# Three partial matmuls of a split product, with the two that use the weights' high part put next to each other

## The chip, the cores and the metric

The kernel runs on one core of a Trainium2 chip. The metric is device time in microseconds; the kernel before takes 951.2 us (median of three runs, 950.86 to 952.58).

## The reference

Sliding-window attention with a distance bias, and a gated feed-forward network behind it, on 8 batches of 576 tokens, 8 heads of 64, d_model 512, d_ff 1536:

```python
scores = scale * q @ k.T + bias          # window of 128, causal
attn   = softmax(scores)
x      = (attn @ v)  -> [4608, 512]
gate   = 1 / (1 + exp(-(x @ w_gate)))
out    = (gate * (x @ w_val)) @ w_out
```

All inputs and outputs are float32.

## The kernel before

**Split products.** The feed-forward matmuls take operands in a rounded 32-bit format that TensorE handles in one pass. To keep float32 accuracy, every operand is cut into two: a high part (the value rounded to that format, written by a copy) and a low part (the value minus its high part, written by a subtraction that reads the high part). A product is then the sum of three matmuls into one PSUM bank: high x high, and the two mixed ones (high part of one operand, low part of the other). The weights are TensorE's stationary operand and the activations its moving one, so each matmul is a pair of instructions: a weight load (PEld in the profile) and the matmul itself (PE).

**Three places** issue such triples. `project` in `gates1` (L695) does the first four of twelve d_ff chunks as a plain product, 8 projections of 4 triples for each of 5 token blocks of 512, in between the attention's own matmuls. `product` in `gates2` (L780) does the other chunks with a seven-product scheme (sums of sub-blocks, buffers cxA, cxB, cxC), 384 or 512 tokens wide. `product` in `results` (L1064) does the out projection with a scheme of 15 products, 512 wide, from four buffers (three in cxA, one in cxC) used in turn.

**Where the parts come from.** `parts` (its copy is recorded at L286 or L287, its subtraction at L296) writes the high part and then the low part. Each is written anew when a new block or sub-block comes, and then has to wait until the matmuls that read the old one are through. `x1` (tile x in the trace) holds one token block for L695; there is one copy of it.

**What sets the order.** Nothing is issued as the code is written. Every step is entered in a `Graph` with an engine, an assumed cost, what it reads and writes and a wish time (`want`). `order` then goes through the entries as a greedy planner: it takes the entry that can start first (in buckets of 0.05 us), among equal ones that with the lower wish time, and so fixes the order in which each engine's instructions are issued. A table (`SHIFTS`) moves the wish times of groups of entries. In `gates2` and `results` the six matmuls of two triples are ONE entry, which reads all four parts:

```python
g.add("PE", 6 * (N / 2400 + 0.0133), six, [("xc", k, 0), ("xc", k, 1), ("w2", i, 0, wa), ("w2", i, 1, wa)], ...
```

In `project` every matmul is an entry of its own, which reads one part of the weights and one of x, with the highest wish time of all (it goes where nothing else can start):

```python
g.add("PE", n / 2400 + 0.014, one, [("w1", kind, wi, i), (("xhi", "xlo")[x], c)], keys_of(s), 1.0e6)
```

Semaphores between engines are put in by the framework, from the instructions as they are issued: each instruction waits for the writers of what it reads itself. TensorE's waits stand on the weight load of the pair.

Of the kernel before, what the change touches and what calls it, by code (L numbers as in the profile page):

```python
# [259 lines left out]
def act_cost(n, psum=False):  # L260
    return (0.05 if psum else 0.1) + n * 0.00084
# [3 lines left out]
def attention_gated_ffn(ctx: ExitStack, tc: tile.TileContext, qd, kd, vd, wg, wv, wo, out):  # L265
# [409 lines left out]
    def gates1(t0, n):  # L675
        F = FIRST
        xr = lambda: xrow()[:, :, 0:n]
        a = t0
        while t0 and a < t0 + n:
            b = a // S  # L680
            e = min((b + 1) * S, t0 + n)
            move(lambda a=a, e=e: xr()[:, :, a - t0:e - t0],
                 lambda b=b, a=a, e=e: xs[b][:, :, a - b * S:e - b * S].rearrange("c p t -> p c t"),
                 [("xs", b, p) for p in range(NPAIR)], [("xr", c, a > t0) for c in range(KC)], F, 2 * (e - a))
            a = e
        for c in range(KC if t0 else 0):
            parts(lambda c=c: x1(0)[:, c, 0:n], lambda c=c: x1(1)[:, c, 0:n], lambda c=c: xr()[:, c], n,
                  [("xr", c, e) for e in range(2)], ("xhi", c), ("xlo", c), F)

        def project(kind, i):  # L690
            s = bank()
            for c in range(KC):
                for k, (wi, x) in enumerate(((0, 0), (1, 0), (0, 1))):
                    def one(c=c, k=k, wi=wi, x=x):
                        nc.tensor.matmul(psum(s)[:, 0:n], w1(kind, wi)[:, i, c * P:(c + 1) * P], x1(x)[:, c, 0:n],  # L695
                                         start=(k == 0 and c == 0), stop=(k == 2 and c == KC - 1))
                    g.add("PE", n / 2400 + 0.014, one, [("w1", kind, wi, i), (("xhi", "xlo")[x], c)], keys_of(s), 1.0e6)
            return s

        for i0 in range(0, FC1, GRP):  # L700
            grp = range(i0, min(FC1, i0 + GRP))
            for i in grp:
                s = project("g", i)
                g.add("ACT", act_cost(n, psum=True), lambda s=s, i=i: nc.scalar.activation(sgate(i % GRP)[:, 0:n], psum(s)[:, 0:n], AF.Tanh, scale=0.5),
                      keys_of(s), [("sg", i % GRP)], F)
            for i in grp:
                s, r = project("v", i), spills[0] % NRING1
                spills[0] += 1
                h = lambda r=r: ring[:, r * NB:r * NB + n]
                g.add("DVE", dve_cost(n, psum=True), lambda s=s, i=i, h=h: nc.vector.scalar_tensor_tensor(  # L710
                    h(), sgate(i % GRP)[:, 0:n], 1.0, psum(s)[:, 0:n], op0=ALU.add, op1=ALU.mult), [*keys_of(s), ("sg", i % GRP)], [("rg1", r)], F)
                spill(h, ("rg1", r), i, t0, n)
# [33 lines left out]
    def gates2(t):  # L746
        F = FIRST + (1 if t else 0.4)
        N, t0 = HALVES[t], EDGE[2 * t]
        xr = lambda: xrow()
        x = lambda h, k: (lambda: xr()[:, 2 * k:2 * k + 2, h * N2:h * N2 + N])  # L750
        for h in range(2):
            a = t0 + h * N
            while a < t0 + (h + 1) * N:
                b = a // S
                e = min((b + 1) * S, t0 + (h + 1) * N)
                move(lambda a=a, e=e, h=h: xr()[:, :, h * (N2 - N) + a - t0:h * (N2 - N) + e - t0],
                     lambda b=b, a=a, e=e: xs[b][:, :, a - b * S:e - b * S].rearrange("c p t -> p c t"),
                     [("xs", b, p) for p in range(NPAIR)], [("xr", k, (h, a > t0 + h * N)) for k in range(2)], F, 2 * (e - a))
                a = e
        xk = {(h, k): [("xr", k, (h, e)) for e in range(2)] for h in range(2) for k in range(2)}  # L760
        m = 2 * N
        mixed = mix(lambda k, val, reads: parts(lambda: combo(k, 0)[:, :, 0:N], lambda: combo(k, 1)[:, :, 0:N], val, m, reads, ("xc", k, 0), ("xc", k, 1), F),
            x, xk, m, F)
        have = set()

        def chunk(i):
            bx, by, bz = bank(), bank(), bank()
            sa, su, sp_ = scratch(), scratch(), scratch()
            a1, u2, p5 = (lambda s=s: ring2(s)[:, 0:N] for s in (sa, su, sp_))
            sg = [lambda h=h: sgate(h)[:, 0:N] for h in range(2)]  # L770
            bk = lambda b: (lambda: mm[b][:, 0:N])

            def product(k, b, start, wk):
                while k not in have:
                    have.add(next(mixed))

                def six():
                    for c in range(2):
                        for j, (xp, wp) in enumerate(((0, 0), (0, 1), (1, 0))):
                            nc.tensor.matmul(mm[b][:, 0:N], w2t(i, wp)[:, wk, c * P:(c + 1) * P], combo(k, xp)[:, c, 0:N],  # L780
                                             start=(start and c == 0 and j == 0), stop=(c == 1 and j == 2), skip_group_check=True)
                wa = 0 if wk < 2 else 2
                g.add("PE", 6 * (N / 2400 + 0.0133), six, [("xc", k, 0), ("xc", k, 1), ("w2", i, 0, wa), ("w2", i, 1, wa)],
                      [("mm", b)], 1.0e6)

            def total(o, b, a, reads, writes, okeys):
                g.add("DVE", dve_cost(N, psum=True), lambda: nc.vector.tensor_tensor(o(), bk(b)(), a(), op=ALU.add),  # L787
                      [("mm", b), *reads] if okeys else reads, writes, F)

            def gate(b, h):  # L790
                g.add("ACT", act_cost(N, psum=True), lambda: nc.scalar.activation(sg[h](), bk(b)(), AF.Tanh, scale=0.5),  # L791
                      [("mm", b)], [("sg", h)], F)

            def gated(o, val, reads, key, h, psum):
                g.add("DVE", dve_cost(N, psum, True), lambda: nc.vector.scalar_tensor_tensor(
                    o(), sg[h](), 1.0, val(), op0=ALU.add, op1=ALU.mult), [("sg", h), *reads], [key], F, port=not psum)
                spill(o, key, chunk_of(i), t0 + h * N, N)

            ka, ku, kp = (("rg", s) for s in (sa, su, sp_))
            product(0, bx, True, 0)  # L800
            copy(a1, bk(bx), N, [("mm", bx)], [ka], F, psum=True)
            yield
            product(3, bz, True, 3)
            copy(p5, bk(bz), N, [("mm", bz)], [kp], F, psum=True)
            yield
            product(4, bx, False, 4)
            copy(u2, bk(bx), N, [("mm", bx)], [ku], F, psum=True)
            yield
            product(1, by, True, 1)
            total(bk(by), by, a1, [ka], [("mm", by)], False)  # L810
            gate(by, 0)
            yield
            product(5, bx, False, 5)
            total(p5, bx, p5, [], [kp], True)
            yield
            product(2, bz, False, 2)
            total(bk(bz), bz, u2, [ku], [("mm", bz)], False)
            gated(u2, bk(bz), [("mm", bz)], ku, 0, True)
            yield
            product(6, bx, False, 6)  # L820
            gate(bx, 1)
            gated(p5, p5, [], kp, 1, False)

        return chunk
# [128 lines left out]
    def results(wsrc):  # L953
# [97 lines left out]
        def product(t, e, k, at):  # L1051
# [6 lines left out]
            for i in two:  # L1058
                b = banks_[z][i]
                for a, c in halves(t, k, i) if e else ((0, NB),):  # L1060
                    def six(b=b, i=i, a=a, c=c):
                        for d in range(2):
                            for j, (xp, wp) in enumerate(((0, 0), (0, 1), (1, 0))):
                                nc.tensor.matmul(mm[b][:, a:c], wot(n, wp)[:, 2 * e + d, i * P:(i + 1) * P], pieces[q](xp)[:, d, a:c],  # L1064
                                                 start=(k in fresh and e == d == j == 0), stop=(e == 1 and d == 1 and j == 2),
                                                 skip_group_check=True)
                    g.add("PE", 6 * ((c - a) / 2400 + 0.0133), six,
                          [("hc", q, 0), ("hc", q, 1), ("wo", n, 0), ("wo", n, 1)] + [("mm", b)] * (a > 0), [("mm", b, 1) if a else ("mm", b)], 1.0e6)
# [3 lines left out]
        for kind, t, e, what, at in plan():  # L1072
            if kind == "wload":
                wsplit(what, at, wsrc)
            elif kind == "load":
                k, b = int(what[1]), int(what[2]) + 3 * t
# [3 lines left out]
            elif kind == "add":  # L1080
                x, y, o = at
# [189 lines left out]
```

## Time and profile before

| | |
|---|---|
| median of three runs | 951.2 us |
| the profiled execution: time, span in the trace | 951.76 us, 949.8 us |
| TensorE: matmuls, weight loads | 6586, 6586 |
| TensorE busy with matmuls, with loads | 941.6 us, 796.4 us |
| VectorE, ScalarE, GpSimd busy | 820.4, 541.4, 153.8 us |

The profiled execution's span is the time from its first to its last instruction; 1.96 us of its time lie around it. A matmul's record runs until its results are out, so consecutive ones overlap, and a mean of some 390 ns is not the distance from one to the next: that is the length of a dense stretch through the matmuls in it. By line and place in time there are three stages: attention with L695 in its gaps (to about 290 us), L780 (to about 700 us), L1064 (to the end).

### The profile page before, as it was taken

How to read it: one execution, taken by the hardware profiler on the slowest of the kernel's cores; microseconds unless marked ns; L12 is line 12 of the kernel's file. 1: busy time of each engine (PE TensorE's matmuls, PEld its weight loads, DVE VectorE, ACT ScalarE, POOL GpSimd, SP SyncE). 2: the span in 40 equal slices, each digit the busy share in tenths (PEclk: the TensorE clock that was granted, in tenths of full speed). 3: DMA queues.
4: the chain of work that ended last, by engine and by line, in shares of the span. 5: the costliest groups of instructions: out<-in, count | busy, mean ns of one | idle time of the engine just before them, and what ended most of it. 6: DMA issues, size and time to landing. Idle time of an engine off the chain costs nothing.

```text
span 949.8 us, 18733 instructions
## 1 busy us (share of the span) xinstructions
PE 941.6 (99%) x6586; PEld 796.4 (84%) x6586; DVE 820.4 (86%) x2022; ACT 541.4 (57%) x1364; POOL 153.8 (16%) x321
## 2 busy tenths in 40 slices
PE   8999999999999999999999999999999999999998
PEld 7888887788888889999988888888888888888886
DVE  7998989986879998796969939895899999999985
ACT  8999988887745654443545425342455435444432
POOL 5665556563400000000001000000000000000000
PEclk9999999999999999999999999999999999999999
DMA  7766768765426436567374422543587795597542
GB/s 265 257 227 231 258 212 274 242 211 194 149 72 210 155 125 207 179 219 242 115 244 167 153 81 72 194 146 132 195 274 256 229 327 174 186 329 245 155 134 89
DMA packets 101294, 185.78 MB, mean 196 GB/s; under 512 B 9680, under 2 KB 37456, under 8 KB 101200
## 3 DMA queue, kind: packets, MB, share of 16 engines
q1 hardware_dynamic: 101200, 184.58, 58.7%
q8 instruction: 52, 0.85, 0.4%
q14 instruction: 42, 0.34, 0.1%
HBM read 128.45 MB, written 56.10 MB: 194 GB/s over the span
## 4 chain that ended last, share of the span: by engine, by line
PE 96%; DVE 1%; DMA 1%; ACT 1%; issue 0%; SPq 0%; POOL 0%; DVEq 0%; ACTq 0%
PE mm L780 44%; PE mm L1064 26%; PE mm L695 12%; PE mm L502 5%; PE mm L643 5%; PE mm L575 4%; PE mm L620 1%; DVE pb L533 1%; PE mm L563 1%; DMA qr<-in_q_dram 0%; ACT pb L536 0%; DMA hs<-ring 0%; DVE mm L512 0%; SPq L291 0%; DVE st L551 0%
## 5 line engine op out<-in xcount | busy, mean ns | idle before, releaser
L286 ACT COPY ring<-mm 128x512 f32<-128x512 f32 (+1 forms) x177 | 97.1, 559 | 165.8 <-PE mm L780 109.6
L695 PE MATMUL mm<-x,wl 128*128 128x512 f32 x480 | 133.6, 410 | 0.0
L589 POOL TENSOR_SCALAR_AFFINE_SELECT pt<-both 128x384 f32<-128x384 f32 (+1 forms) x256 | 114.9, 479 | 96.2 <-ACT both L286 83.3
L780 PE MATMUL mm<-cxB,wh 128*128 128x512 f32 (+1 forms) x504 | 117.1, 374 | 0.2 <-ACT ring L286 0.2
L780 PE MATMUL mm<-cxA,wh 128*128 128x512 f32 (+1 forms) x504 | 117.2, 374 | 0.0
L536 ACT ACTIVATE pb<-pb,st 128x128 f32<-128x128 f32 x288 | 112.5, 394 | 5.2 <-DVE st L533 5.0
L780 PEld LDWEIGHTS mm<-cxB,wh 128*128 128x128 f32 x504 | 92.7, 188 | 14.5 <-ACT ring L286 0.5
L780 PEld LDWEIGHTS mm<-cxA,wh 128*128 128x128 f32 x504 | 92.7, 188 | 14.2 <-DVE wh L296 0.2
L695 PEld LDWEIGHTS mm<-x,wl 128*128 128x128 f32 x480 | 84.2, 188 | 18.4 <-issue 2.2
L1064 PE MATMUL mm<-cxA,wl 128*128 128x512 f32 x416 | 99.2, 389 | 0.0
L791 ACT ACTIVATE sg<-mm 128x512 f32<-128x512 f32 (+1 forms) x96 | 53.7, 564 | 75.8 <-PE mm L780 48.2
L1064 PE MATMUL mm<-cxA,wh 128*128 128x512 f32 (+1 forms) x384 | 94.4, 387 | 0.0
L1064 PEld LDWEIGHTS mm<-cxA,wl 128*128 128x128 f32 x416 | 78.1, 188 | 16.2
L787 DVE TENSOR_TENSOR mm<-mm,ring 128x512 f32<-128x512 f32 (+1 forms) x96 | 62.1, 650 | 28.2 <-PE mm L780 21.1
L1064 PEld LDWEIGHTS mm<-cxA,wh 128*128 128x128 f32 x384 | 71.9, 188 | 14.7
L780 PE MATMUL mm<-cxB,wl 128*128 128x512 f32 (+1 forms) x360 | 82.4, 367 | 0.0
L780 PE MATMUL mm<-cxA,wl 128*128 128x512 f32 (+1 forms) x360 | 81.9, 367 | 0.0
L780 PEld LDWEIGHTS mm<-cxB,wl 128*128 128x128 f32 x360 | 65.9, 188 | 8.6
L780 PEld LDWEIGHTS mm<-cxA,wl 128*128 128x128 f32 x360 | 65.8, 188 | 8.6
L420 DVE SCALAR_TENSOR_TENSOR work<-work 128x512 int32<-128x512 int32 x104 | 71.6, 702 | 0.4
L502 PE MATMUL mm<-kr,qr 64*64 64x192 f32 (+2 forms) x1408 | 61.4, 304 | 0.9 <-DMA qr<-in_q_dram 0.9
L502 PEld LDWEIGHTS mm<-kr,qr 64*64 64x64 f32 x1408 | 49.2, 133 | 9.9 <-issue 4.6
(143 smaller groups left out, 1665.7 us busy)
## 6 DMA issues: line engine op xcount, KB each, us to landing
hs<-ring SPq DMA_DIRECT2D x84, 256.0 KB, 2.4
hb<-hs SPq DMA_DIRECT2D x38, 512.0 KB, 5.3
work<-hs SPq DMA_DIRECT2D x29, 512.0 KB, 4.6
kr<-in_k_dram SPq DMA_DIRECT2D x31, 384.0 KB, 4.4
xr<-hs SPq DMA_DIRECT2D x23, 512.0 KB, 5.4
work<-in_moe_w_gate_dram SPq DMA_DIRECT2D x20, 512.0 KB, 4.2
work<-in_moe_w_val_dram SPq DMA_DIRECT2D x20, 512.0 KB, 4.4
qr<-in_q_dram SPq DMA_DIRECT2D x31, 320.0 KB, 5.0
```

Source lines behind the costliest of these rows:

```text
L286: g.add("ACT", act_cost(n, psum), lambda: nc.scalar.copy(out(), src()), reads, writes, want, release=release, guard=guard, ways=[("DVE", d ...
L420: g.add("DVE", dve_cost(DM, two=True), lambda word=word, scalar=scalar, o0=o0: nc.vector.scalar_tensor_tensor(bits(), wraw(s)[:, :, word], ...
L502: nc.tensor.matmul(sp[v.at][col, j, c0:c0 + n], qraw(u)[row, i // 2, col], kraw(u)[row, k1:k1 + n], start=True, stop=True)
L536: g.add("ACT", 0.39, lambda: nc.scalar.activation(pb()[:, e], pb()[:, e], AF.Exp, bias=st()[:, e:e + 1], scale=-1.0, accum_out=st()[:, 3 + ...
L575: nc.tensor.transpose(tp[:, e], pb()[:, e], ident)
L589: nc.gpsimd.affine_select(pt(u)[:, f0:f0 + 2 * m_ - 1:2, h * D:h * D + D], both().rearrange("p a (h q) -> p (a h) q", q=D)[:, c0:c0 + m_], ...
L643: nc.tensor.matmul(to[e * D:(e + 1) * D], vraw(u)[row, c], seen[row, o + t0:o + t1], start=(k, e) not in begun, stop=jj + 2 > NBLK - 1, sk ...
L695: nc.tensor.matmul(psum(s)[:, 0:n], w1(kind, wi)[:, i, c * P:(c + 1) * P], x1(x)[:, c, 0:n], start=(k == 0 and c == 0), stop=(k == 2 and c ...
L780: nc.tensor.matmul(mm[b][:, 0:N], w2t(i, wp)[:, wk, c * P:(c + 1) * P], combo(k, xp)[:, c, 0:N], start=(start and c == 0 and j == 0), stop ...
L787: g.add("DVE", dve_cost(N, psum=True), lambda: nc.vector.tensor_tensor(o(), bk(b)(), a(), op=ALU.add), [("mm", b), *reads] if okeys else r ...
L791: g.add("ACT", act_cost(N, psum=True), lambda: nc.scalar.activation(sg[h](), bk(b)(), AF.Tanh, scale=0.5), [("mm", b)], [("sg", h)], F)
L1064: nc.tensor.matmul(mm[b][:, a:c], wot(n, wp)[:, 2 * e + d, i * P:(i + 1) * P], pieces[q](xp)[:, d, a:c], start=(k in fresh and e == d == j ...
```

## The change

In each of the three places the second and the third matmul of a triple change places. Before, the weights of the three are high, low, high, and the activations high, high, low. After, the weights are high, high, low, and the activations high, low, high. The same three products are summed into the same bank; the counts of instructions as written are the same.

```diff
         def project(kind, i):
-                for k, (wi, x) in enumerate(((0, 0), (1, 0), (0, 1))):
+                for k, (wi, x) in enumerate(((0, 0), (0, 1), (1, 0))):
...
                 def six():                                   # gates2
-                        for j, (xp, wp) in enumerate(((0, 0), (0, 1), (1, 0))):
+                        for j, (xp, wp) in enumerate(((0, 0), (1, 0), (0, 1))):
...
                     def six(b=b, i=i, a=a, c=c):             # results
-                            for j, (xp, wp) in enumerate(((0, 0), (0, 1), (1, 0))):
+                            for j, (xp, wp) in enumerate(((0, 0), (1, 0), (0, 1))):
```

(`wi` and `wp` pick the part of the weights, `x` and `xp` that of the activations; 0 is the high part.)

## Rows read from the trace of the kernel before

**Rows 1.** The page: busy time by engine; granted clock in 40 slices.
```profile
PE 941.6 (99%) x6586; PEld 796.4 (84%) x6586; DVE 820.4 (86%) x2022; ACT 541.4 (57%) x1364; POOL 153.8 (16%) x321
...
PEclk9999999999999999999999999999999999999999
```

**Rows 2.** The page: the chain that ended last, by engine and line.
```profile
PE 96%; DVE 1%; DMA 1%; ACT 1%; issue 0%; SPq 0%; POOL 0%; DVEq 0%; ACTq 0%
PE mm L780 44%; PE mm L1064 26%; PE mm L695 12%; PE mm L502 5%; PE mm L643 5%; PE mm L575 4%; PE mm L620 1%; DVE pb L533 1%; PE mm L563 1%; DMA qr<-in_q_dram 0%; ACT pb L536 0%; DMA hs<-ring 0%; DVE mm L512 0%; SPq L291 0%; DVE st L551 0%
```

**Rows 3.** Stretches: busy us of each engine (instructions), granted clock, DMA share.
```profile
60.00:290.00 230.00, 230.00 (x2858) 186.03 (x2857) 197.40 (x940) 190.71 (x710) 114.57 (x244) 1.00 0.63 207
290.00:700.00 410.00, 409.84 (x1964) 358.69 (x1963) 340.85 (x566) 187.00 (x316) 3.75 (x2) 1.00 0.50 166
700.00:950.00 250.00, 246.06 (x1092) 203.79 (x1090) 230.32 (x231) 109.11 (x132) 0.00 (x0) 1.00 0.66 219
```

**Rows 4.** Waits of the matmuls: us in total, times, longest.
```profile
PE mm L780 <- ACT ring L286: 0.2, 1, 0.2
```

**Rows 5.** Stretches inside the two product stages, columns as in Rows 3.
```profile
740.00:840.00 100.00, 100.00 (x443) 82.80 (x442) 95.48 (x96) 44.89 (x55) 0.00 (x0) 1.00 0.73 239
390.00:440.00 50.00, 49.84 (x288) 49.52 (x287) 45.44 (x89) 22.27 (x44) 0.00 (x0) 1.00 0.63 208
```

**Rows 6.** The whole span, lines 695, 780 and 1064 each alone.
```profile
0.00:950.00 950.00, 133.57 (x480) 84.18 (x480) 1.00 0.59 196
0.00:950.00 950.00, 422.14 (x2016) 368.72 (x2016) 1.00 0.59 196
0.00:950.00 950.00, 245.03 (x1086) 203.15 (x1086) 1.00 0.59 196
```

**Rows 7.** Line 355 alone: duration min/median/max ns, first and last start.
```profile
L355 PEld LDWEIGHTS mm<-ident x40: 186/192/333, 3.1 to 18.0; 128*128 128x128 f32 x40
L355 PE MATMUL mm<-ident x40: 275/275/421, 3.3 to 18.1; 128*128 128x128 f32 x40
```

**Rows 8.** Tile x, 36 to 290 us: idle ahead of its loads, times.
```profile
  DVE x L296: 0.7, 2
...
  DVE wl L296: 0.2, 1
```

**Rows 9.** In order of time, 47.8 to 49.9 us: start, us, engine, line.
```profile
47.46 2.62 PE L695 MATMUL mm<-x,wl 128*128 128x512 f32 x10
...
47.72 0.42 DVE L287 CAST x<-xt 128x512 fp32r<-128x512 f32 x1
...
48.17 1.00 DVE L296 TENSOR_TENSOR x<-xt,x 128x512 fp32r<-128x512 f32 x1
```

**Rows 10.** In order of time, 160.5 to 163.2 us.
```profile
160.74 1.97 DVE L296 TENSOR_TENSOR x<-xr,x 128x512 fp32r<-128x512 f32 x2
...
161.31 2.20 PE L695 MATMUL mm<-x,wl 128*128 128x512 f32 x7
...
161.83 0.53 PEld L695 LDWEIGHTS mm<-x,wl 128*128 128x128 f32 x3 [0.25 <-DVE x L296]
...
162.76 0.53 PEld L695 LDWEIGHTS mm<-x,wl 128*128 128x128 f32 x3 [0.41 <-DVE x L296]
```

**Rows 11.** In order of time, 406.4 to 408.6 us.
```profile
406.48 0.95 DVE L296 TENSOR_TENSOR cxA<-xr,cxA 128x768 fp32r<-128x768 f32 x1
...
407.72 1.05 PEld L780 LDWEIGHTS mm<-cxA,wl 128*128 128x128 f32 x6
```

**Rows 12.** In order of time, 809.4 to 811.8 us.
```profile
808.44 1.05 ACT L286 CAST cxA<-xr 128x1024 fp32r<-128x1024 f32 x1 [2.32 <-PE mm L1064]
...
809.52 1.23 DVE L296 TENSOR_TENSOR cxA<-xr,cxA 128x1024 fp32r<-128x1024 f32 x1 [0.53 <-ACT cxA L286]
...
811.41 0.41 PEld L1064 LDWEIGHTS mm<-cxA,wl 128*128 128x128 f32 x2
```

**Rows 13.** ScalarE's waits, 700 to 950 us: us in total, times, longest.
```profile
ACT cxA L286 <- PE mm L1064: 51.0, 34, 6.0
```

## The prediction

> **What bounds the kernel now.** I read the page first. The busy line gives TensorE 99% with matmuls and 84% with weight loads, and 6586 of each: every matmul has a load of its own. The clock line says full speed (2.4 GHz) in all 40 slices [rows 1]. The chain of waits is TensorE for 96% of the span, 82% of it in the three lines of the change: L780 44%, L1064 26%, L695 12% [rows 2]. So a nanosecond per matmul there is a nanosecond of the kernel, and nothing on another engine counts unless it makes TensorE late.
>
> A busy TensorE need not be a dense one, so I looked next at distances. In a hundred microseconds of L1064 there are 442 loads, one per 226 ns; in fifty of L780 at 384 columns 288 matmuls, one per 174 ns [rows 5]. The columns alone take 512/2.4 = 213 and 384/2.4 = 160 ns. So each pair costs its columns and 13 to 14 ns, whatever its width, while a load (188 ns as a record: 82.80 us over 442 [rows 5]) is otherwise hidden beside the matmul before it. VectorE is at 230 of 250 us in the last stage [rows 3], yet TensorE's waits show a single one in both product stages, 0.2 us [rows 4]: from 290 us on the stream is dense. L695 is not: 133.57 us for 480 matmuls, 278 ns each [rows 6], 52 ns over the dense 226. That is 25 us lost at the changes between it and the attention's matmuls.
>
> **The change, part by part.** How many neighbours: a third of the matmuls of L695, L780 and L1064, (480 + 2016 + 1086)/3 = 1194 as instructions [rows 6]. These come to share their weights with the one before.
>
> *Weight loads.* The diff asks for matmuls and never for loads, so the question is whether a repeated load falls away by itself. The nearest row is line 355, the warm-up: 40 matmuls whose weights are all the same identity tile, and 40 loads of 186 ns or more [rows 7]. That speaks for loads that stay. It is not quite the same case, since those matmuls are of another type, in which one matmul of the code becomes two instructions. I take 0 saved; the other end, all of the 13 ns gone for 1194 matmuls, is 15.5 us, and no row suggests that a repeated load costs more than a new one.
>
> The Trainium skill speaks for that other end. "TensorE: Matmul & The Clock Gate", section "Step-by-step: what each phase is for", says that weights usually stay in place over many matmuls and that loading is an instruction of its own so that one load can serve several; its section "Back-to-back issue gap" gives a lone matmul of 512 columns about 216 ns. By that rule 1194 matmuls would each be about 10 ns shorter, some 12 us in all, as an estimate from the page. Line 355 goes against its first half, as far as it applies.
>
> *L780 and L1064: parts that are needed earlier or come free later.* In the planner the six matmuls are one entry with the same operands as before, so these two stages are dealt as now. On the chip the low part of the activations is needed one matmul earlier (174 to 226 ns), the low part of the weights one later; the high part of the activations comes free one matmul later. The last counts where a copy waits for it: 34 copies of L1064's stage do [rows 13]. In such a case both add up: release 226 later, use 226 earlier, 0.45 us of room lost. The closest that I found: in L1064 a copy that waited for TensorE at 808.44, its subtraction from 809.52 to 810.75, and the load that first needs it at 811.41, 0.66 us of room [rows 12]; in L780 a subtraction to 407.43 and its load, the third from 407.72 on, at about 408.07, 0.64 us [rows 11]. After the change about 0.2 us is left in each. I take 0; if the tightest fell short, it would be by tenths of a microsecond a time. The cover is the distance between the splits and the matmuls; were it gone, each of the 90 pieces of the out projection (15 products, 3 groups of tokens, 2 halves) could cost up to 0.45 us, 40 us in all, which these rows exclude.
>
> *L695: stalls.* Here there is one x1, written anew between blocks, so splits are late by design: the low part is what L695's loads wait for, 0.7 us in two places, and the low weights 0.2 us in one [rows 8]. The two stand at 161.83 and 162.76 [rows 10], behind 2 us of subtractions. There are 5 blocks x 4 low parts = 20 such first uses. If each were one matmul earlier and each high part one matmul later on the path, that is 20 x 0.45 = 9 us, the upper end; the lower end is the 0.2 us for the weights that goes away. The row that it is nearest to is the two waits seen: two or three places late by 0.23 us more, 0.7, less 0.2, so +0.5 us.
>
> *L695: the order.* This part is the uncertain one. In `project` every matmul is an entry with its own operands, and the planner now learns that the second of a triple needs the low part. In the first block that changes its answer: the copy of the fourth piece starts at 47.72, its subtraction runs from 48.17 to 49.17, and the run of ten L695 matmuls around them began at 47.46 [rows 9]; the second matmul of that triple, which used only the high part, could go about a microsecond earlier than it now can. Once one entry moves, the greedy choice among attention, L695 and the other engines' work can come out otherwise from there to about 290 us. All the work stays the same, and the number of changes between L695 and the attention's matmuls may rise or fall. What that can cost is bounded by what those changes cost now, 25 us; nothing says which way it goes, and I take 0, with a tenth of it, 2.5 us, as an ordinary deviation to either side.
>
> *Sum.* Against the profiled execution's 951.76 us (span 949.8 and 1.96 around it): 0 + 0 + 0.5 + 0 = 952.3. This execution is 0.6 us above the median of the runs, so against the median of 951.2 the forecast is 951.7; I write 951.8. What a measurement of this kernel can tell from no change is about 0.2%, 1.9 us.
>
> **The rivals.**
> *Slower: a worse dealing of the attention stage.* Place: 41 to 290 us. Mechanism: low parts that the planner sees as late break L695's triples apart, and each break is one more change between kinds of matmul. It decides from about 1.4 us on top of the 0.5, which is 6% more than the 25 us. At a fifth more it is 951.2 + 0.5 + 5 = 956.7, at an eighth 954.8, and I put it at 954.5. For it: triples were in one piece because the first two matmuls needed only the high part, and splits do come just in time [rows 10]. Against it: from the third block on most low parts seem to be long there, since only two waits are seen.
> *Faster: a better dealing.* The same mechanism the other way, 2.5 to 3 us less: 948.5. For it: the low weights, which also came late once, may now come last.
> *Faster: the repeated loads, or their 13 ns, fall away.* 951.2 - 15.5 = 935.7 if all of it goes. For it: 13 ns are there on every pair, and the order puts equal weights side by side. Against it: line 355.
> *Slower: stalls in the product stages* after all, if a copy that comes later pushes VectorE, at 92% there, behind. At 0.2 us for 15 of the 90 pieces 3 us: 954.7. I count it with the first.
>
> **How the numbers follow.** No change that can be measured, 951.8: 0.53. Worse dealing or stalls: 0.30. Better dealing: 0.11. Loads gone: 0.06. So faster 0.17, same 0.53, slower 0.30. The range leaves out the loads (0.06) and the outer parts of the two dealings (some 0.06 each side): 947.5, a good 3.5 us below, to 956.5, the fifth more. The likeliest case has 949.3 to 953.1 as its own range.
>
> **What would show it.** Loads: 6586 of them again, and 226 and 174 ns a pair in the same two stretches; fewer loads, or 213 and 160 ns, and the third rival holds. Products: TensorE's waits still near 0.2 us behind 290 us; a row of L780 or L1064 waiting for the low part of cxA, cxB or cxC would be the stalls. Stalls of L695: the wait for x at L296 rises from 0.7 us to little over 1. Order: the moment when the first L780 matmul starts tells the whole of the dealing, and L695's busy time of 133.57 us a part of it; over 136 is the slower rival. The prediction is wrong if the product stages, 290 us to the end, change their length by over half a microsecond, or if the attention stage does by more than 2.

## The result, and the profile after

The changed kernel takes 965.3 us (median of four runs, 963.57 to 965.79) against 951.89 for the kernel before (four runs): a ratio of 1.0136, 95% interval 1.0116 to 1.0156, slower by 1.4%, 13.4 us. That is outside the range of 947.5 to 956.5.

The page of the kernel after, its busy line, the granted clock and the chain of waits, against [rows 1, 2]:

```profile
PE 949.3 (99%) x6586; PEld 798.4 (83%) x6586; DVE 825.1 (86%) x2018; ACT 536.9 (56%) x1361; POOL 154.2 (16%) x328
...
PEclk9999999999999999999999999999999999999989
...
PE 93%; DVE 3%; ACT 1%; DMA 1%; issue 0%; SPq 0%; POOL 0%; DVEq 0%; ACTq 0%
```

The loads are all there, 6586 of them. What is new stands beside TensorE: VectorE has 3% of the chain where it had 1%, the clock falls in one slice near the end, and the counts on VectorE, ScalarE and GpSimd are not those of before (2022, 1364, 321). The diff touches none of these engines.

Where the time went, by the first and the last start of the out projection's matmuls and the first of L780. The answers for L780 and L1064, before:

```profile
L780 PE MATMUL mm<-cxA,wl x360: 333/389/397, 278.9 to 665.4; 128*128 128x512 f32 x108, 128*128 128x384 f32 x72
...
L1064 PE MATMUL mm<-cxA,wl x416: 389/389/389, 701.0 to 904.8; 128*128 128x512 f32 x139
L1064 PE MATMUL mm<-cxA,wh x384: 277/389/389, 731.2 to 945.8; 128*128 128x512 f32 x188, 128*128 128x256 f32 x4
```

and after:

```profile
L780 PE MATMUL mm<-cxA,wl x360: 333/389/398, 284.3 to 671.2; 128*128 128x512 f32 x108, 128*128 128x384 f32 x72
...
L1064 PE MATMUL mm<-cxA,wl x416: 387/389/454, 706.7 to 920.0; 128*128 128x512 f32 x139
L1064 PE MATMUL mm<-cxA,wh x384: 278/389/793, 737.1 to 959.6; 128*128 128x512 f32 x188, 128*128 128x256 f32 x4
...
L1064 PE MATMUL mm<-cxA,w x22: 279/389/389, 783.4 to 959.7; 128*128 128x512 f32 x18, 128*128 128x256 f32 x4
```

The two times behind the durations are first and last start. The attention stage ends 5.4 us later (284.3 for 278.9). From there L780 takes 422.4 us for 422.1 until L1064 starts. The last stage takes 253.0 us (706.7 to 959.7) for 244.8 (701.0 to 945.8), 8.2 more. The three make up the 13.9 us by which the span grew (963.7 less 949.8). Of the 5.4 us, 2.3 are waits of matmuls that the kernel before does not have there (1.4 us of L575, 0.9 of L695); the rest is not taken apart here.

Inside the product stages the dense stretches are as they were [rows 5], in windows with the same columns:

```profile
740.00:840.00 100.00, 100.00 (x443) 82.63 (x442) 95.56 (x95) 45.45 (x54) 0.00 (x0) 1.00 0.72 234
390.00:440.00 50.00, 50.00 (x290) 50.00 (x289) 45.09 (x86) 21.48 (x44) 0.00 (x0) 1.00 0.59 200
```

442 loads in 100 us, again 226 ns a pair: a pair whose weights are already there takes as long as any other. By the start times of single matmuls of 512 columns that follow another of the three lines directly, 931 whose weights are those of the matmul before start 227 ns after it, and 1869 others 227 ns (medians).

The matmuls' waits, where [rows 4] had one short wait behind 290 us:

```profile
PE mm L1064 <- DVE cxC L296: 1.8, 1, 1.8
...
PE mm L1064 <- DVE mm L978: 0.7, 1, 0.7
PE mm L1064 <- ACT cxC L286: 0.7, 1, 0.7
PE mm L1064 <- ACT ring L286: 0.7, 1, 0.7
...
PE mm L780 <- DVE ring L795: 0.6, 1, 0.6
```

The wait of L780 lies at 508 us; the four of L1064 lie close together, between 909 and 928 us. In order of time, after (start, duration, engine, line; the wait in brackets):

```profile
909.69 0.59 ACT L286 COPY ring<-mm 128x512 f32<-128x512 f32 x1 [7.10 <-PE mm L1064]
909.69 0.69 DVE L287 CAST cxA<-work 128x1024 fp32r<-128x1024 f32 x1 [1.41 <-PE mm L1064]
910.33 1.23 PEld L1064 LDWEIGHTS mm<-cxA,wh 128*128 128x128 f32 x6 [1.10 <-ACT ring L286]
...
918.71 1.22 DVE L1084 TENSOR_TENSOR hb<-work 128x1024 f32<-128x1024 f32 x1
919.85 1.22 DVE L296 TENSOR_TENSOR cxA<-xr,cxA 128x1024 fp32r<-128x1024 f32 x1
919.96 1.05 ACT L286 CAST cxC<-hb 128x1024 fp32r<-128x1024 f32 x1 [1.69 <-DVE hb L1084]
...
920.98 1.22 DVE L1084 TENSOR_TENSOR hb<-hb,work 128x1024 f32<-128x1024 f32 x1
921.06 0.19 PEld L1064 LDWEIGHTS mm<-cxC,wh 128*128 128x128 f32 x1 [1.11 <-ACT cxC L286]
...
922.12 1.22 DVE L296 TENSOR_TENSOR cxC<-hb,cxC 128x1024 fp32r<-128x1024 f32 x1
...
923.39 3.17 PEld L1064 LDWEIGHTS mm<-cxC,wh 128*128 128x128 f32 x11 [2.14 <-DVE cxC L296]
...
928.00 4.02 PEld L1064 LDWEIGHTS mm<-cxA,wh 128*128 128x128 f32 x11 [1.44 <-DVE mm L978]
```

VectorE makes the sum hb at 918.71, ScalarE can only then write its high part (919.96), VectorE does two other things first and subtracts at 922.12, and TensorE's loads stand for 1.1 and then 2.1 us. At 928.00 they have stood for 1.4 us more for a subtraction of VectorE's. The wait at 910.33 is of another kind: there ScalarE copies out a bank that TensorE had only just filled. And the stall costs twice, as the stretches around it show (columns as in [rows 3]):

```profile
905.00:920.00 15.00, 14.32 (x63) 11.26 (x61) 11.73 (x13) 2.86 (x5) 0.00 (x0) 1.00 0.50 163
920.00:925.00 5.00, 2.48 (x10) 1.48 (x9) 5.00 (x5) 1.95 (x2) 0.00 (x0) 0.98 0.40 121
925.00:930.00 5.00, 4.28 (x11) 2.88 (x10) 5.00 (x8) 1.04 (x1) 0.00 (x0) 0.50 0.00 0
930.00:935.00 5.00, 5.00 (x20) 4.03 (x19) 3.79 (x4) 1.62 (x2) 0.00 (x0) 0.84 0.51 154
```

VectorE is busy in all of 920 to 930; TensorE was busy for 2.48 us between 920 and 925, and then its clock is granted at 0.50, the lower level of 1.2 GHz. In the 6.8 us at that level (0.2, 5 and 1.6 by the shares) dense matmuls start 427 ns apart instead of 227, so thirteen of them come 0.2 us later each, 2.6 us. The waits ahead of L1064's loads are 2.1 + 1.4 + 1.1 + 1.1 = 5.7. Together that is about 8.3, for the 8.2 by which the stage grew.

So VectorE is late where nothing of VectorE's was edited. The waits of VectorE from 700 us on, before:

```profile
DVE ring L978 <- PE mm L1064: 7.9, 4, 6.6
DVE cxA L287 <- PE mm L1064: 4.1, 5, 2.1
```

and after:

```profile
DVE cxA L287 <- PE mm L1064: 9.0, 8, 3.1
DVE ring L978 <- PE mm L1064: 6.3, 3, 5.4
```

In a stage where it is busy for 92% it now stands 9.0 us instead of 4.1 in front of copies into buffers that TensorE still reads, with sums and subtractions queued behind. Between 888 and 919 us, just ahead of the stall, VectorE has seven copies of high parts, four of which wait for TensorE (0.8, 0.8, 1.4 and 0.4 us); before it had three there, none with a wait. That is a matter of which instructions stand in its queue, and in which order. Set side by side, the orders of instructions of the two kernels differ on all five engines, from the first block of L695 on.

### The profile page after: what moved, and what is told of

Read it like the earlier page. It is cut to its first block, busy times and chain, and to the rows that moved or that the text cites. A ratio compares the mean times of both kernels' runs of the same rounds, so it can differ in the third digit from the quotient of the medians.

```text
span 963.7 us, 18693 instructions
## 1 busy us (share of the span) xinstructions
PE 949.3 (99%) x6586; PEld 798.4 (83%) x6586; DVE 825.1 (86%) x2018; ACT 536.9 (56%) x1361; POOL 154.2 (16%) x328
## 4 chain that ended last, share of the span: by engine, by line
PE 93%; DVE 3%; ACT 1%; DMA 1%; issue 0%; SPq 0%; POOL 0%; DVEq 0%; ACTq 0%
PE mm L780 44%; PE mm L1064 25%; PE mm L695 11%; PE mm L502 5%; PE mm L643 4%; PE mm L575 3%; DVE pb L533 1%; PE mm L620 1%; DMA work<-in_moe_w_gate_dram 1%; ACT pb L536 1%; PE mm L563 1%; DMA qr<-in_q_dram 0%; DVE hb L1084 0%; DVE mm L512 0%; DVE work L420 0%
## 5 line engine op out<-in xcount | busy, mean ns | idle before, releaser
L695 PE MATMUL mm<-x,wl 128*128 128x512 f32 x480 | 134.3, 411 | 0.9 <-DVE ring L710 0.9
L589 POOL TENSOR_SCALAR_AFFINE_SELECT pt<-both 128x192 f32<-128x192 f32 (+1 forms) x256 | 112.9, 472 | 87.4 <-ACT both L286 77.2
L780 PE MATMUL mm<-cxB,wh 128*128 128x512 f32 (+1 forms) x504 | 117.6, 374 | 0.6 <-DVE ring L795 0.6
L780 PE MATMUL mm<-cxA,wh 128*128 128x512 f32 (+1 forms) x504 | 117.2, 373 | 0.0
L780 PEld LDWEIGHTS mm<-cxB,wh 128*128 128x128 f32 x504 | 92.6, 188 | 15.3 <-DVE ring L795 1.0
L780 PEld LDWEIGHTS mm<-cxA,wh 128*128 128x128 f32 x504 | 92.8, 188 | 13.9
L695 PEld LDWEIGHTS mm<-x,wl 128*128 128x128 f32 x480 | 84.1, 188 | 19.3 <-issue 1.7
L1064 PE MATMUL mm<-cxA,wl 128*128 128x512 f32 x416 | 99.6, 389 | 0.0
L1064 PE MATMUL mm<-cxA,wh 128*128 128x512 f32 (+1 forms) x384 | 96.3, 393 | 1.4 <-DVE mm L978 0.7
L1064 PEld LDWEIGHTS mm<-cxA,wl 128*128 128x128 f32 x416 | 78.0, 188 | 16.4 <-DVE cxA L296 0.2
L1064 PEld LDWEIGHTS mm<-cxA,wh 128*128 128x128 f32 x384 | 72.9, 191 | 17.9 <-DVE mm L978 1.4
L780 PE MATMUL mm<-cxB,wl 128*128 128x512 f32 (+1 forms) x360 | 82.9, 367 | 0.0
L780 PE MATMUL mm<-cxA,wl 128*128 128x512 f32 (+1 forms) x360 | 82.0, 367 | 0.0
L780 PEld LDWEIGHTS mm<-cxA,wl 128*128 128x128 f32 x360 | 65.8, 188 | 8.6
L780 PEld LDWEIGHTS mm<-cxB,wl 128*128 128x128 f32 x360 | 65.9, 188 | 8.5
```

The source lines that it names most:

```text
L589: nc.gpsimd.affine_select(pt(u)[:, f0:f0 + 2 * m_ - 1:2, h * D:h * D + D], both().rearrange("p a (h q) -> p (a h) q", q=D)[:, c0:c0 + m_], ...
```

## The experiments

Theory A: three matmuls in another order cost nothing on the chip; the planner, told in L695 that the second of a triple reads another part, deals everything behind anew, to the end of the kernel, and worse. Rival B: parts needed earlier and freed later stall the engines. Rival C: shared weights change the price of a pair. Rival D: the loss comes in proportion to the triples turned round. Rival E: only late low parts are dealt badly. Each ratio below is to the kernel before, run beside it on the same chip (medians of 951.2 to 952.8 us).

**The plan and the order on the chip, apart from each other.** Two kernels separate what the planner is told (`planned`) from what is issued. In both, the order of instructions on every engine but TensorE is that of the kernel whose plan they have.

```diff
-                for k, (wi, x) in enumerate(((0, 0), (0, 1), (1, 0))):
+                triples[0] += 1
+                planned = ((0, 0), (1, 0), (0, 1))
+                issued = planned if triples[0] - 1 in (3, 93, 95, 121, 125) else ((0, 0), (0, 1), (1, 0))
+                for k, ((rw, rx), (wi, x)) in enumerate(zip(planned, issued)):
...
-                    g.add("PE", n / 2400 + 0.014, one, [("w1", kind, wi, i), (("xhi", "xlo")[x], c)], keys_of(s), 1.0e6)
+                    g.add("PE", n / 2400 + 0.014, one, [("w1", kind, rw, i), (("xhi", "xlo")[rx], c)], keys_of(s), 1.0e6)
```

This is the edit of the first kernel; in the second the two orders are exchanged and the list is `(12,)`. The triples listed keep the planned order, since their other part isn't written yet, or not any more, at that place of the plan. (Triples are counted from 0.) The first kernel has the new order in L695, L780 and L1064 and the old plan:

> All three lines issue their matmuls in the new order (155 of L695's 160 triples, all of L780's and L1064's), but the planner is told L695's old operands, so that every engine's other instructions stand in the order of before. Theory A (the loss is the order that the planner deals once it is told the new operands, not the order of three matmuls on the chip): within 0.3% of before, 949 to 955 us, and first L780 matmul at 279 us. Rival B (the low part needed one matmul earlier, the high part free one later, stall TensorE): 960 us or more, with waits for low parts at L296 in the product stages. Rival C (a repeated load is dearer or cheaper than a new one): dense stretches off 226 ns a pair; 13 ns less for a third of the pairs would give 936.

It took 951.28 us, ratio to before 0.9991 (0.9981 to 1.0002). L780 begins at 278.6:

```profile
L784 PE MATMUL mm<-cxA,wl x360: 332/389/398, 278.6 to 664.6; 128*128 128x512 f32 x108, 128*128 128x384 f32 x72
```

No matmul of the product lines is among its waits, and the waits of L695's loads for low parts of x are 0.8 us in two places, for 0.7 in two before [rows 8]; they have one new wait for a high part, 0.3 us, and no longer the 0.2 us for the weights. The second kernel is the reverse:

> The planner is told L695's new operands, but the matmuls are issued in the old order (weights high, low, high) in 159 of L695's 160 triples and all of L780's and L1064's: no two neighbours share weights. Theory A: the changed kernel's time, 962 to 968 us, first L780 matmul near 284 us, a last stage of some 257 us. Rivals B and C: 949 to 955 us.

965.96 us, ratio 1.0142 (1.0126 to 1.0158), with the old order in all triples but one. Stage by stage it is the kernel after, with a last stage of 251.4 us (707.1 to 958.5; the expectation said some 257):

```profile
L784 PE MATMUL mm<-cxA,wl x360: 333/389/398, 284.6 to 671.5; 128*128 128x512 f32 x108, 128*128 128x384 f32 x72
...
L1068 PE MATMUL mm<-cxA,wh x384: 278/390/499, 737.2 to 958.5; 128*128 128x512 f32 x188, 128*128 128x256 f32 x4
```

So the whole loss goes with the plan, and B and C fall: 1189 triples in the new order changed the time by 0.2% at most.

**The edit by parts.** The product lines alone (the two lower hunks of the diff), and `project` alone (the upper one):

> L780 and L1064 in the new order, L695 as before. Theory A: these two are one entry per six matmuls, so the plan is unchanged: 949 to 955 us. Rival B: most splits are in these stages, so most of the loss, 958 us or more, in the last stage above all.

952.72 us, ratio 1.0000 (0.9986 to 1.0014).

> L695 alone in the new order, L780 and L1064 as before. Theory A: all of the loss, 962 to 968 us, most of it after 900 us although nothing there was edited. Rival B: under a third of it, 956 us at most.

965.88 us, ratio 1.0141 (1.0126 to 1.0156). L780 begins at 286.4 us and the last matmul of L1064 starts at 960.3, with TensorE's longest wait, 1.6 us, again for cxC in L1064, a line that is as before in this kernel. The expectation had most of the loss after 900 us; here some half of it lies ahead of L780. The kernel after issues the same instructions in the same order up to there and began L780 at 284.3, so single executions of one dealing differ by 2 us in the attention stage.

**How little it takes.** One triple of L695, number 4, told to the planner and issued in the new order:

```diff
+                planned = ((0, 0), (0, 1), (1, 0)) if triples[0] - 1 == 4 else ((0, 0), (1, 0), (0, 1))
+                issued = planned
```

> The kernel before, with ONE triple of its 1194 in the new order: L695's second projection of the first block, first quarter of the columns summed over. It is the one whose second matmul had to wait for the weights' low part (47.80 us in the trace of before) and now asks for x's low part, which is there by then. Theory A (any small move of an entry makes the greedy planner deal the rest anew, and its table of wish times fits one dealing only): 957 us or more, losses in stages where nothing was edited. Rival D (the loss comes from what the new order itself asks for, in proportion to the triples turned round): 951 to 953 us, since one triple is under 0.1% of them.

964.89 us, ratio 1.0137 (1.0122 to 1.0152). Another one, number 12:

> The kernel before, with one other triple in the new order: L695's fourth projection of the first block, first quarter. Theory A: slower again, but by another amount than with the first triple, since it is another dealing: 960 to 980 us. Rival D: 951 to 953 us.

979.37 us, ratio 1.0289 (1.0270 to 1.0309): twice the loss of the whole edit, with waits in L780 too, which the kernel after hardly has:

```profile
PE mm L784 <- ACT ring L286: 6.0, 4, 4.2
PE mm L784 <- ACT sg L795: 3.2, 2, 2.7
PE mm L1068 <- DVE cxC L296: 2.7, 2, 1.8
```

The two expectations describe them wrongly in one point: both kernels had L780 and L1064 in the new order as well, as in the run of the product lines alone. So the first was run once more without that:

> The kernel before with one triple turned round and nothing else: L695's second projection of the first block, first quarter. (In the two earlier runs with one triple of L695, L780 and L1064 had the new order as well.) Theory A: the same time as there, 962 to 968 us. If the two product lines had a part in that loss: under 960 us.

965.11 us, ratio 1.0141 (1.0127 to 1.0155). One triple of 1194 has the loss of the whole edit, with the same mark on VectorE:

```profile
DVE cxA L287 <- PE mm L1068: 8.6, 8, 3.1
DVE ring L982 <- PE mm L1068: 7.2, 5, 5.4
```

D falls. The opposite of it is the whole edit without four triples of L695, the two above and two of the fourth block:

```diff
+                planned = ((0, 0), (0, 1), (1, 0)) if triples[0] - 1 not in (4, 12, 121, 125) else ((0, 0), (1, 0), (0, 1))
+                issued = planned
```

> The changed kernel with four of its 1194 triples left in the old order: in L695, the first quarter of the second and of the fourth projection of the first block, and two quarters of the last-but-one and last projection of the fourth block, the ones whose own entry moves when it is turned round. 1190 triples have the new order, told to the planner and issued. Theory A: as before, 949 to 955 us, first L780 matmul at 279 us. Rival D: 964 us or a little less. Rival C, a gain from shared weights without a bad dealing: 936 to 942 us.

951.16 us (11 runs), ratio 1.0000 (0.9991 to 1.0008). 1190 triples in the new order, told and issued, and nothing lost or gained. The expectation is not quite right that only the four move: the second matmul of triple 3 is planned 0.9 us later here as well (49.5 for 48.6 us), but the order closes up behind it, and only a handful of entries on each engine stand elsewhere than before. So a moved entry need not upset what follows. Its dense stretches:

```profile
740.00:840.00 100.00, 100.00 (x442) 82.79 (x442) 95.30 (x96) 45.50 (x54) 0.00 (x0) 1.00 0.72 240
390.00:440.00 50.00, 50.00 (x290) 50.00 (x289) 45.07 (x88) 21.98 (x44) 0.00 (x0) 1.00 0.63 211
```

**No new order at all.** Only an assumed cost is changed:

```diff
-                    g.add("PE", n / 2400 + 0.014, one, ...
+                    g.add("PE", n / 2400 + 0.0141, one, ...
```

> The kernel before, all triples in the old order; only the cost that the planner assumes for a matmul of L695 is 0.1 ns higher (0.014 to 0.0141 us per matmul). Nothing of the work or of what depends on what is changed. Theory A: slower by 1 to 2%, 958 to 970 us, as if the order of the triples had been changed. Rival D, and rival E (the planner's answer is only bad for late low parts): 950 to 954 us.

964.51 us, ratio 1.0138 (1.0123 to 1.0154). E falls too: the planner's answer gets as much worse when a number in it moves by 0.1 ns.

**What the planner itself expected.** `order` gives every entry a start, so each kernel has a planned end of its last matmul that needs no chip:

| kernel | planned end | more than before | measured ratio |
|---|---|---|---|
| before | 944.8 us | | |
| the whole edit, `project` alone | 957.3 | 12.5 | 1.0136, 1.0141 |
| triple 4 | 957.7 | 12.9 | 1.0137, 1.0141 |
| triple 12 | 970.1 | 25.3 | 1.0289 |
| 0.1 ns of cost | 956.9 | 12.1 | 1.0138 |
| all but four, the product lines alone | 944.8 | 0.0 | 1.0000 |

In the plan of the whole edit L780 begins at 283.1 us for 278.4, and the last stage takes 252.0 us for 244.9. The loss stands in the plan itself, at nearly its measured size; it is not a good plan that meets the chip badly.

**A table for the new order.** The changed kernel with `SHIFTS` searched anew (470 entries differ), the search looking only at when the planner expects the last matmul:

> The changed kernel, all triples in the new order, with the table of wish times (SHIFTS) searched anew for its own dependences. Theory A: the loss goes away, 949 to 954 us, last stage back to 245 us and at full clock. If the new order cost something by itself, 958 us or more would stay.

955.33 us, ratio 1.0041 (1.0026 to 1.0055); two thirds of the loss are gone, not all of it as expected (954 us at most). The last stage is back, 704.3 to 949.0, 244.7 us, and no matmul of L780 or L1064 waits:

```profile
L784 PE MATMUL mm<-cxA,wl x360: 333/389/397, 282.0 to 668.7; 128*128 128x512 f32 x108, 128*128 128x384 f32 x72
...
L1068 PE MATMUL mm<-cxA,wl x416: 389/389/389, 704.3 to 908.1; 128*128 128x512 f32 x139
...
L1068 PE MATMUL mm<-cxC,wh x124: 388/389/389, 742.9 to 949.0; 128*128 128x512 f32 x124
```

The attention stage is not: L780 begins at 282.0, for 278.9 before. Another search:

> The changed kernel with another table of wish times, from a search with other random numbers that ended at the same planned time. Theory A: 949 to 957 us; the last stage without waits, and the rest decided by how well the dealing of the attention stage meets the chip, which the planner does not know to the microsecond.

955.68 us, ratio 1.0048 (1.0033 to 1.0064), L780 from 281.4 on. What keeps the attention stage 2.5 to 3 us longer under both tables is open. The planner does not see it: its planned ends are 945.1 and 945.7 us, 0.3 and 0.8 more than before, and it has L780 begin at 279.1 under both. What is left is a difference between the planned times and the chip's, which no run here takes apart. No kernel here beats the one before.

## Why the prediction was wrong, point by point

*What bounds the kernel.* Right as far as the runs go: matmuls that came 0.2 us later each made the last stage longer by their sum, and VectorE counted where it made TensorE late. No run made a pair cheaper.

*Weight loads, 0 saved.* Right: the same count and the same 226 ns, with and without a neighbour's weights. The rule quoted from the Trainium skill ("TensorE: Matmul & The Clock Gate", "Step-by-step: what each phase is for"), one load for several matmuls, does not come about by itself here: 6586 loads for 6586 matmuls, and the measurement decides. A matmul without a load of its own, at that page's 216 ns, is shown by no run.

*L780 and L1064, parts needed earlier or freed later: 0.* Right as a price on the chip: the product lines alone gave 1.0000 (0.9986 to 1.0014), with no wait of a product matmul in its trace, so the room that was left in the tight places was enough.

*L695, stalls: +0.5.* Too much, but small: with the old plan and the new order the loads' waits for x are 0.8 and 0.3 us instead of 0.7, and the 0.2 for the weights is gone, 0.2 more in all.

*The step that failed is the sentence on the product stages, "so these two stages are dealt as now".* It took the entries' operands for what fixes the dealing. The operands were the same, but the planner is one list from the first instruction to the last: what it knows of the engines when it comes to L780 and L1064, and so what it puts next into each queue, hangs on everything dealt before. 8.2 of the 13.9 us were lost in L1064, and the run with `project` alone lost 6.6 there. In the sum it is the last term, the order, that was put at 0 because "nothing says which way it goes": the planner's own end does say it, 12.5 us later. The rival "a worse dealing" had the right mechanism, a chance of 0.30 and the wrong size: it was confined to 41 to 290 us, priced by the 25 us lost between kinds of matmul, and so ended at 954.5. Within its place it was a fair guess in size alone: that stage lost 5.4, but not in the 25 us it was priced by (L695's busy time is 134.31 for 133.57). The rival of stalls in the product stages named VectorE and the place rightly, at 3 us, but by another way: copies that come free later. With the old plan the same matmuls stalled nowhere there.

*The "tenth of it, 2.5 us, as an ordinary deviation to either side"* failed as well. Nothing in the profile could show the size; the planned end could, and the table of several hundred wish times could have warned that it belongs to one dealing. The four dealings tried that differ widely from before and had no search of their own (the whole edit, triple 4, triple 12, 0.1 ns of cost) are all slower, by 1.4 to 2.9%; the one of the kernel with 1190 triples, which differs little, gave 1.0000. No faster side showed. The four are not independent draws: the last 83 of TensorE's planned entries stand in the same order in all of them, and each trace has a wait of 1.6 to 1.8 us for cxC there, so much of the loss in the last stage is one loss met four times.

*The place* was half right. The triple of the fourth piece, split from 47.72 us on [rows 9], does move in the plan, but it is among the 1190 triples that do no harm. Triple 4 is the first of the second projection; its second matmul had waited for the weights' low part, which is the 0.2 us wait of [rows 8] that the prediction had entered as a small gain.

*The signs* named showed it in part: first L780 matmul at 284 instead of 279, the last stage longer. L695's busy time, which was to pass 136 us, stayed at 134.31. And the wait for the low part of cxC, which was to mean stalls from the new order, came from the dealing.

## What to carry to other kernels

Where a greedy planner orders a kernel, an edit of one entry can be an edit of everything behind it (triple 4), though it need not be (1190 other triples), and a table of priorities found by search may be worth little once the dealing has changed. So look first at the planner's own planned end before and after, compare the issue order on all engines, not the lines of the diff, and search again before judging the edit. To learn what an edit costs on the chip, hold the plan and change what is issued, and the other way round; two runs then say which of the two it was. A late engine can be late through an instruction far ahead of it in its queue that waits for a buffer, so look at that engine's own waits.

## What the runs showed of the hardware

Two neighbours with the same weights are as far apart as two with different ones, 227 ns at 512 columns, and each has its own load: the 13 ns over the columns stay. TensorE was busy for 2.48 us between 920 and 925 us; its clock was then granted at 0.50 from 925 to 930, and the waits of 5.7 us in the last stage brought 2.6 us more through matmuls at 1.2 GHz, which start 427 ns apart.
